# Attention output left transposed, its factors spread by loads through DRAM, dummy transposes ahead of the first layer norm, and a table of due times in the scheduler of an Infini-attention and GEGLU kernel

## The chip, the core and the metric

The kernel runs on one core of a Trainium2 chip. A core has five engines, each with its own queue of instructions executed in order: TensorE (PE in the profile, its weight loads PEld), VectorE (DVE), ScalarE (ACT), GpSimd (POOL) and SyncE (SP, which here only issues DMA). They synchronise by semaphores. PE writes to PSUM, which has eight banks of 128 partitions x 512 words of float32. The metric is the device time of one execution in microseconds; lower is better.

## The reference

One transformer layer over 2048 tokens of width 512: attention with 32 heads of 16 in four segments of 512 tokens with a memory that is carried from segment to segment, then a gated feed-forward of width 1376, each behind a layer norm and with a residual.

```python
for s in range(4):                     # segments
    logits = q_s @ k_s.T * 0.25 + mask # causal, per head
    a_dot = softmax(logits) @ v_s
    pq = phi(q_s)                      # phi(t) = t + 1 if t > 0 else exp(t)
    a_mem = (pq @ M) / (pq @ z + 1e-6)
    o_s = g * a_mem + (1 - g) * a_dot  # g = sigmoid(beta), one per head
    M += phi(k_s).T @ v_s;  z += phi(k_s).sum(0)
h = x + o @ wo
out = h + (gelu(ln(h) @ w_gate) * (ln(h) @ w_up)) @ w_down
```

## The kernel before, in words

The heads are worked on in four chunks of eight (`c`), the tokens in four segments (`s`). A pair is a unit `U`; there are 16, in the order of `UNITS`: all chunks of segments 0 and 1 first, then of 2 and 3. Each unit is worked on in two halves `Q` of four heads. What needs the float32 precision is split into two float32r parts, so a product is three matmuls (`SPLIT`).

The program is written as a list of operations, each with an engine, an estimated duration, a priority `prio` (a due time: the lowest goes first) and the tiles that it reads and writes. `Sched.run` goes through a modelled time, picks for each engine what is ready first, among those within a small window the one with the lowest `prio`, and so fixes the order of every engine's instructions; pools (`Pool_`) hand out tiles and PSUM banks in that order. The chip then executes these orders and waits on semaphores where the model was wrong. Before the change every `prio` is a formula in `U`, `Q` or `s`, such as `2 * U + (-2.08)`, and a DMA is modelled by a fixed delay (`lat`) behind its issue.

- `ln1(s)` loads four tiles of x (L517) and normalises them (`layer_norm`): for segments 0 and 1 on DVE (L450 to L471), for 2 and 3 with the sums on ACT (L436, L445). The result is transposed by PE (L497) and split by ACT and DVE (L506, L507) into `xt`.
- `qkv(U)` projects q and k (L536) and v (L565), copies q and k out of PSUM (L594, L596) and moves them by DMA into the layout of the score matmuls: `stq` (L609) and `stk` (L615). These buffers are first filled with zeros and ones by POOL and ACT (`c_fill` at L360, `c_stk` at L378 and L381). For segments 0 to 2 the keys' feature map goes, transposed (L632), into the memory product (L640), masked into `mb` (L643).
- `mem(U)`, for segments 1 to 3 (12 units): PE multiplies the memory with the queries (L664; tokens on partitions, 8 heads x 17 columns, the 17th being the denominator), DVE adds 1e-6, takes the reciprocal, multiplies by the gate and scales (L671 to L681) into `om`.
- `pass_a(Q)`: scores (L701) and their row maxima (DVE, L711), which go by DMA into a row of `stq` (L739). `pass_b(Q)`: transposed scores (L756) minus the maxima, exponentials on ACT (L760), causal masks on POOL (L764), and the product with v in four 32-column tiles of the array side by side (L785), which leaves in bank `pv` the result transposed: heads and their 16 values on partitions (the 17th row of each is the softmax sum), tokens on columns. ACT copies it out (`pvs`, L804), PE transposes it back in four transposes (L808), DVE takes the reciprocal of the sums, multiplies by 1 - g and scales (L820 to L824), POOL adds `om` (L829), and SP stores 128 KB to `o_dram`, token rows in runs of 256 bytes (L835).
- `wo_seg(s)` loads four tiles of `o_dram` and of x (L850, L851), transposes the first (L855), splits it (L506, L507), multiplies it with wo (L862), adds x on DVE (L866) and stores the residual (L868). Its operations' `prio` is `27.83 + 1.924 * s`, in the units of `U` and `Q`.
- The second layer norm and the feed-forward (L1031, L1092 on PE, weights prepared by ACT and POOL at L999 to L1008) fill the rest. From about 500 us on there is nothing else.

## Time and profile before

| | |
|---|---|
| Runs, us | 852.15, 851.84, 849.77; median 851.84 |
| Profiled execution, own time | 850.29 us |
| Its span (first to last instruction) | 848.2 us |
| Busy: PE, DVE, ACT, POOL | 825.0, 621.8, 511.7, 458.7 us |
| Share of 16 DMA engines, queue of SP | 34.8% |
| DMA moved | 82.9 MB, 64179 packets, 25056 of them under 512 bytes |

A row of the groups names the line, the engine, the operation, output and inputs, shapes, the number of instructions, then busy time and mean ns of one, then the idle time of the engine just before them and what ended it. A piece of the chain is start, length, and what it was. Matmuls overlap, so the mean of one is its latency and not the time that it adds. A float32 matmul stands as two records in the trace, a float32r one or a transpose as one.

### The profile page before, as it was taken

Reading aid. Unit: us, or ns where it says so; the run is one execution under the profiler, and the core shown is the slowest. Engines: PE = TensorE matmul, PEld = TensorE weight load, DVE = VectorE, ACT = ScalarE, POOL = GpSimd, SP = SyncE. Lnnn points to the kernel's source line nnn. Section 1 sums busy time; section 2 is a strip of 40 time slices with the busy share of each in tenths; the row PEclk is TensorE's granted clock in tenths of the full one; section 3 lists DMA queues with packets and bytes.
Section 4 is the critical chain, followed back from the end, with each engine's and each line's share of the span. In section 5 each row is a group of like instructions: output and inputs, shape, how many; then the busy total and the mean of one; then the engine's idle time right before and its main releaser. Section 6 shows DMA issues by size and latency. Waiting matters only on the chain.

```text
span 848.2 us, 15681 instructions
## 1 busy us (share of the span) xinstructions
PE 825.0 (97%) x4924; PEld 656.3 (77%) x4924; DVE 621.8 (73%) x1963; ACT 511.7 (60%) x966; POOL 458.7 (54%) x791
## 2 busy tenths in 40 slices
PE   4899999999999999999999999999999999999998
PEld 4787777877788777887777688788888877788886
DVE  7788877779867778868698675565666885756656
ACT  6767667578755666557445763774656764636441
POOL 6433534434335453445333673588878767779650
PEclk9999999999999999999999999999999999999999
DMA  7444432444344333243343464422212351122102
GB/s 248 120 119 96 96 74 69 108 103 96 85 121 122 89 85 97 48 121 90 107 122 122 126 230 143 122 72 63 63 51 62 119 158 38 50 63 62 51 1 100
DMA packets 64179, 82.90 MB, mean 98 GB/s; under 512 B 25056, under 2 KB 27040, under 8 KB 64096
## 3 DMA queue, kind: packets, MB, share of 16 engines
q1 hardware_dynamic: 64096, 81.91, 34.8%
q8 instruction: 39, 0.64, 0.3%
q14 instruction: 44, 0.36, 0.2%
HBM read 43.14 MB, written 12.58 MB: 66 GB/s over the span
## 4 chain that ended last, share of the span: by engine, by line
PE 92%; DVE 4%; ACT 2%; issue 1%; DMA 1%; SPq 0%; POOL 0%; ACTq 0%; DVEq 0%; POOLq 0%
PE bank L1031 24%; PE bank L1092 14%; PE bank L536 10%; PE bank L701 9%; PE bank L756 9%; PE bank L785 8%; PE bank L862 5%; PE bank L565 4%; PE bank L497 2%; PE bank L808 2%; PE bank L664 1%; PE bank L640 1%; PE bank L632 1%; PE bank L855 1%; ACT pt L760 1%
## 5 line engine op out<-in xcount | busy, mean ns | idle before, releaser
L711 DVE CUSTOM_DVE_ANT_0 junk<-bank,amask 128x256 f32<-128x256 f32 (+3 forms) x512 | 231.0, 486 | 54.1 <-PE bank L701 49.8
L764 POOL TENSOR_SCALAR_AFFINE_SELECT pt<-pt 128x128 f32<-128x128 f32 (+1 forms) x448 | 131.8, 314 | 202.5 <-ACT pt L760 192.1
L760 ACT ACTIVATE pt<-bank 128x512 f32<-128x512 f32 x320 | 177.8, 602 | 63.0 <-PE bank L756 50.4
L701 PE MATMUL bank<-stk,stq 128*128 128x512 f32 (+2 forms) x384 | 130.5, 386 | 0.9 <-DVE nm L711 0.5
L756 PE MATMUL bank<-stq,stk 128*128 128x384 f32 (+3 forms) x512 | 119.8, 325 | 1.3 <-ACT pt L760 0.8
L536 PE MATMUL bank<-xt,w 128*128 128x512 f32 x384 | 109.2, 397 | 0.0
L756 PEld LDWEIGHTS bank<-stq,stk 128*128 128x128 f32 x512 | 85.8, 189 | 15.4 <-ACT pt L760 6.2
L1097 DVE TENSOR_TENSOR pt<-pt,bank 128x512 f32<-128x512 f32 x96 | 64.9, 685 | 28.7 <-PE bank L1092 28.3
L701 PEld LDWEIGHTS bank<-stk,stq 128*128 128x128 f32 x384 | 66.8, 189 | 19.5 <-issue 9.3
L536 PEld LDWEIGHTS bank<-xt,w 128*128 128x128 f32 x384 | 70.0, 189 | 10.9
L785 PE MATMUL bank<-pt,vaug 128*32 128x512 f32 (+3 forms) x1024 | 76.0, 436 | 0.0
L785 PEld LDWEIGHTS bank<-pt,vaug 128*32 128x32 f32 x1024 | 28.4, 109 | 39.9 <-issue 31.8
L1001 POOL TENSOR_TENSOR w<-raw,w 128x512 fp32r<-128x512 f32 (+2 forms) x36 | 42.4, 1180 | 25.4 <-ACT w L999 24.1
L394 POOL TENSOR_TENSOR w<-raw,w 128x512 fp32r<-128x512 f32 (+1 forms) x26 | 34.1, 1312 | 40.6 <-ACT w L389 24.0
L1031 PE MATMUL bank<-xt,stk 128*128 128x512 f32 (+1 forms) x189 | 53.0, 394 | 0.3 <-ACT pq L1038 0.3
L565 PE MATMUL bank<-wv,xt 128*128 128x256 f32 x384 | 52.7, 284 | 0.0
L565 PEld LDWEIGHTS bank<-wv,xt 128*128 128x128 f32 x384 | 50.6, 190 | 1.1
L1031 PE MATMUL bank<-xt,w 128*128 128x512 f32 (+1 forms) x183 | 50.8, 391 | 0.0
L1001 POOL TENSOR_TENSOR stk<-raw,stk 128x512 fp32r<-128x512 f32 (+3 forms) x32 | 36.9, 1155 | 20.1 <-ACT stk L999 19.7
L804 ACT ACTIVATE pvs<-bank 128x512 f32<-128x512 f32 x32 | 19.2, 598 | 44.9 <-PE bank L785 44.9
L1031 PE MATMUL bank<-stk,w 128*128 128x512 f32 (+1 forms) x162 | 45.5, 392 | 0.0
L711 DVE DVE_READ_ACCUMULATOR2_ANT nm<- 128x1 f32 x512 | 42.2, 82 | 0.0
(271 smaller groups left out, 1731.3 us busy)
## 6 DMA issues: line engine op xcount, KB each, us to landing
stq<-hl SPq DMA_DIRECT2D x96, 128.0 KB
stk<-hl SPq DMA_DIRECT2D x192, 64.0 KB
row<-x SPq DMA_DIRECT2D x24, 256.0 KB
raw<-wg SPq DMA_DIRECT2D x20, 256.0 KB
raw<-wu SPq DMA_DIRECT2D x20, 256.0 KB
raw<-wd SPq DMA_DIRECT2D x20, 256.0 KB
o_dram<-o SPq DMA_DIRECT2D x32, 128.0 KB
row<-o_dram SPq DMA_DIRECT2D x16, 256.0 KB
```

What stands on the lines that cost most here:

```text
L536: nc.tensor.matmul(pm.t, w.t[:, wi, dc * P:(dc + 1) * P], XT[s][dc].t[:, xi, :], start=dc == 0 and n == 0, stop=dc == ND - 1 and n == 2)
L565: nc.tensor.matmul(pm.t[:, 256 * t:256 * t + 256], XT[s][dc].t[:, xi, t0:t0 + P], whl[wi].t[:, h, 256 * (dc % 2):256 * (dc % 2) + 256], st ...
L701: nc.tensor.matmul(sa.t[:, k * w:(k + n) * w].rearrange("x (n w) -> x n w", n=n), sq.t[:, p, i * P:(i + 1) * P], sk.t[:, p, a:a + n, 0:w], ...
L711: nc.vector.tensor_tensor_reduce(out=junk.t[:, :w], in0=sa.t[:, k * w:(k + 1) * w], in1=amask[:, D - w:], op0=OP.add, op1=OP.min, scale=-1 ...
L756: nc.tensor.matmul(sc.t[:, lo:lo + D - q0], sk.t[:, p, a, q0:q0 + P], sq.t[:, p, q0:D], start=True, stop=True)
L760: act(D, prio, lambda: nc.scalar.activation(e.t, sc.t, AF.Exp), [sc], [e])
L764: nc.gpsimd.affine_select(v, v, pattern=pat + [[1, P]], compare_op=OP.is_ge, fill=0.0, base=0, channel_multiplier=-1)
L785: nc.tensor.matmul(pv.t[32 * n:32 * n + 32, kb * P:D], va.t[:, kb, 17 * j:17 * j + 32], e.t[:, lo:lo + D - kb * P], start=kb == 0, stop=la ...
L1001: pool(0.14 + 2.13e-3 * (hi - lo), prio, lambda: nc.gpsimd.tensor_tensor(v.t[:, 1, :hi - lo], r.t[:, lo:hi], v.t[:, 0, :hi - lo].bitcast(F ...
L1031: nc.tensor.matmul(dst.t[:w], v.t[:, wi, c0 + j * w:c0 + (j + 1) * w], b[bk][j].t[:, xi, :], start=first and j == 0 and n == 0, stop=j == ...
L1092: nc.tensor.matmul(pm.t, HH[p, f, s][hi].t[:w, t * P:(t + 1) * P], v.t[:w, wi, :], start=f == fl[0] and n == 0, stop=f == fl[-1] and n == 2)
L1097: dve(D, prio, lambda a=a, pm=pm: nc.vector.tensor_tensor(a.t, a.t, pm.t, op=OP.add), [pm], [a])
```

## The change

**The result stays transposed.** ACT's copy of `pv` (`pvs`) is stored to DRAM for each half (L861). After the second half two loads bring back, for all eight heads, the 16 values of each on 128 partitions (`n`, 256 KB) and the sums in a small tile (`cd`) (L867). DVE takes the reciprocal of the sums and multiplies by 1 - g; SP stores them (L876) and a load with a stride of zero spreads each head's row over 16 partitions into `r` (`spread`, L736). POOL multiplies and, for segments 1 to 3, adds `om`; the tile is stored to `o_dram`, now transposed too (L883). `wo_seg` loads it as it is and splits it by ACT and POOL; there are no transposes left in either place. The rows of wo and beta are put in the matching order on the host.

**The memory read likewise.** One group of four 32-column matmuls gives the denominators (`den`, L713), DVE makes the factors (L718 to L720), they are stored and spread (L723, L736), one matmul of 512 columns gives the numerators with the tokens on columns (L729), which waits for the spread factors by the list of its inputs; DVE multiplies (L731). The mask of the memory product writes its columns in two pieces (`mask`).

**Dummy transposes.** 17 transposes of the fourth tile of x (L555) stand ahead of the first layer norm's on PE; nobody reads them. The fills of the third and fourth `stk` buffer wait for the second layer norm (`vcalm[1]`) instead of the first v projection.

**The scheduler.** The model of a transfer now lays transfers one behind another by size (`ring`) and holds SP when eight are outstanding. The pools change: `row` from 6 to 4 tiles, `o` and `cc` go, `n`, `r`, `cd`, `z` come. A table `DUE` holds 216 numbers, by unit, half or segment, that are added to the due times of q, k, v, the moves, the memory read, both passes, the accumulation, the output and the projection. So nearly every engine's order changes.

```diff
+DUE = {
+    "q": [0.25, 2.625, -4, 1, -1.25, 1.375, -0.625, -4, 0.25, -1.25, 2.125, 0.75, 0, 0.875, 0, 1.125],
...
+            if o.eng == "SP":
+                ring = max(ring, end) + o.lat
+                o.lat = ring + 1.5 - end
+                landed.append(ring + 1.5)
+                free["SP"] = max([end] + landed[-8:-7])
...
-        prio = 2 * UNIT[0, s] + (-4.21)
+        prio = 2 * UNIT[0, s] + (-4.21) + DUE["l"][s]
...
+        if s == 0:
+            wm = Val(PB)
+            pe(17 * 2 * TR, prio, lambda: [nc.tensor.transpose(
+                wm.t[:, (n % 4) * P:(n % 4 + 1) * P], rows[3].t[:, (n % 4) * P:(n % 4 + 1) * P],
+                ident) for n in range(17)], [rows[3], vident], [wm])
...
-        for n in range(2):
-            pm, cc = Val(PD), Val(PCC)
-            def f(n=n, pm=pm):
-                for t in range(2):
-                    nc.tensor.matmul(pm.t[:, 136 * t:136 * t + 136],
-                                     pq.t[:, (2 * n + t) * P:(2 * n + t + 1) * P], mb.t,
-                                     start=True, stop=True)
...
+        def den():
+            for t in range(4):
+                nc.tensor.matmul(pd.t[32 * t:32 * t + 32, 0:P], mb.t[:, P:160],
+                                 pq.t[:, t * P:(t + 1) * P], start=True, stop=True,
+                                 tile_position=(0, 32 * t), skip_group_check=True)
+        def inv():
+            nc.vector.tensor_scalar(pd.t[:, 0:P], pd.t[:, 0:P], 1e-6, None, op0=OP.add)
+            nc.vector.reciprocal(pd.t[:, 0:P], pd.t[:, 0:P])
+            nc.vector.tensor_scalar(z.t, pd.t[:, 0:P], gt[:, 1, c:c + 1], None, op0=OP.mult)
+        dma(prio, lambda: nc.sync.dma_start(
+            r_dram[U, 1].rearrange("j (t q) -> t j q", t=4), z.t[0:P:4]), [z], [vr], kb=16)
+        spread(prio, r, U, 1, vr)
+        pe(0.87, prio, lambda: nc.tensor.matmul(pm.t, mb.t[:, 0:P], pq.t, start=True, stop=True),
+           [pq, mb, r], [pm], acq=[om])
+        dve(D, prio, lambda: nc.vector.tensor_tensor(om.t, pm.t, r.t, op=OP.mult), [pm, r], [om])
+    def spread(prio, r, U, i, vr):
+        src = r_dram[U, i]
+        dma(prio, lambda: nc.sync.dma_start(r.t, bass.AP(
+            tensor=src.tensor, offset=src.offset, ap=[[0, 16], [D, 8], [1, D]])), [vr], [r], dur=0.67)
...
-        pe(4 * TR, prio, tr, [pvs, vident], [pn], acq=[cc, o])
+        dma(prio, lambda: nc.sync.dma_start(pv_dram[U, half], pvs.t), [pvs], [OUT[U]], chain=True)
+        if half == 0:
+            return
+        for first, ap, kb in ((16 * D, [32, 16], 24), (0, [D, 16], 256)):
+            dma(prio, lambda first=first, ap=ap: nc.sync.dma_start((cd if first else o).t, bass.AP(
+                tensor=src.tensor, offset=src.offset + first,
+                ap=[ap, [32 * D, 8], [1, ap[0]]])), [OUT[U]], [cd if first else o], kb=kb, dur=0.67)
+        def inv():
+            nc.vector.reciprocal(cd.t, cd.t)
+            nc.vector.tensor_scalar(cd.t, cd.t, gt[:, 0, c:c + 1], None, op0=OP.mult)
+        spread(prio, r, U, 0, vr)
+        pool(1.24, prio, lambda: nc.gpsimd.tensor_tensor(o.t, o.t, r.t, op=OP.mult), [r], [o])
+        if s:
+            pool(1.24, prio, lambda: nc.gpsimd.tensor_tensor(o.t, o.t, OM[U].t, op=OP.add),
+                 [OM[U]], [o])
...
-            pe(4 * TR, prio, tr, [ro, vident], [pt], acq=[ot])
-            split_psum(prio, pt, ot)
+            act(D, prio, lambda ro=ro, ot=ot: nc.scalar.activation(ot.t[:, 0], ro.t, AF.Copy), [ro],
+                [ot], src=0.092)
+            pool(1.23, prio, lambda ro=ro, ot=ot: nc.gpsimd.tensor_tensor(
+                ot.t[:, 1], ro.t, ot.t[:, 0].bitcast(F32), op=OP.subtract), [ro], [ot])
...
-            c_stk(2, [VA[0]])
-            c_stk(3, [VA[0]])
+            c_stk(2, [vcalm[1]])
+            c_stk(3, [vcalm[1]])
```

Three places show how the orders move. The first is ACT at the program's start, before: `xt` is what the first projection reads, `row_98` the first tile of x of segment 2, `stk_88` a buffer that is filled.

```order
L389 ACTIVATE w_82<-raw_105 128x512
L407 ACTIVATE wv_85<-raw_106 128x512
L378 ACTIVATE stk_88<-one 64x2x512
L506 ACTIVATE xt_73<-bank_65 128x512
L506 ACTIVATE xt_74<-bank_66 128x512
L506 ACTIVATE xt_75<-bank_67 128x512
L506 ACTIVATE xt_76<-bank_68 128x512
L378 ACTIVATE stk_88<-one 64x2x512
L436 ACTIVATE junk_118,bn_154<-row_98 128x512
```

And the same place of ACT now:

```order
L422 ACTIVATE w_82<-raw_103 128x512
L440 ACTIVATE wv_85<-raw_104 128x512
L469 ACTIVATE junk_116,bn_152<-row_98 128x512
L411 ACTIVATE stk_88<-one 64x2x512
L539 ACTIVATE xt_73<-bank_65 128x512
L539 ACTIVATE xt_74<-bank_66 128x512
L539 ACTIVATE xt_75<-bank_67 128x512
L539 ACTIVATE xt_76<-bank_68 128x512
L411 ACTIVATE stk_88<-one 64x2x512
```

The sum over `row_98` moved from behind the four copies to ahead of them, and with it ahead of a fill. The second place is POOL around the fills of the third and fourth `stk` (89 and 90), before:

```order
L369 MEMSET amask 128x512
L370 AFFINE_SELECT amask<-amask 128x128
L394 TENSOR_TENSOR w_83<-raw_105,w_83 128x512
L394 TENSOR_TENSOR w_84<-raw_106,w_84 128x512
L381 MEMSET stk_89 64x2x512 x2
L381 MEMSET stk_90 64x2x512 x2
L394 TENSOR_TENSOR w_81<-raw_104,w_81 128x512
```

And now, where `tick` is a one-column copy that waits for the normalised tile `pt_115`:

```order
L402 MEMSET amask 128x512
L403 AFFINE_SELECT amask<-amask 128x128
L427 TENSOR_TENSOR w_83<-raw_103,w_83 128x512
L427 TENSOR_TENSOR w_84<-raw_104,w_84 128x512
L562 COPY tick<-pt_115 128x1
L414 MEMSET stk_89 64x2x512 x2
L414 MEMSET stk_90 64x2x512 x2
```

The fills stand at the same place of POOL's queue, but behind an instruction that waits for the second normalisation. The third place is the memory read of the fourth unit (`mb_138` before, `mb_140` now) on PE, before:

```order
L756 MATMUL bank_70<-stq_94,stk_90 128x384
L756 MATMUL bank_70<-stq_94,stk_90 128x128
L701 MATMUL bank_69<-stk_88,stq_92 128x512
L701 MATMUL bank_68<-stk_88,stq_92 128x512
L664 MATMUL bank_67<-mb_138,pq_122 128x136 x2
L756 MATMUL bank_71<-stq_94,stk_90 128x384
L756 MATMUL bank_71<-stq_94,stk_90 128x128
```

Now on PE, from the denominators (L713) to the numerators (L729); what is left out between is the rest of the accumulation L838 and the scores of both passes:

```order
L576 MATMUL bank_65<-xt_75,w_81 128x512 x3
L713 MATMUL bank_66<-pq_120,mb_140 32x128 x4
L838 MATMUL bank_72<-pt_106,vaug_134 32x512
...
L809 MATMUL bank_70<-stq_94,stk_90 128x384
L809 MATMUL bank_70<-stq_94,stk_90 128x128
L729 MATMUL bank_66<-pq_120,mb_140 128x512
L809 MATMUL bank_71<-stq_94,stk_90 128x256 x2
```

And the transfers of that unit in SP's queue now:

```order
L663 DMA stq_93<-amask 4x4x256
L723 DMA r_dram<-z_129 4x8x128
L861 DMA pv_dram<-pvs_123 128x512
L736 DMA r_125<-r_dram 128x1x512
L883 DMA o_dram<-n_124 128x4x128
L652 DMA stq_94<-hl_95 32x2x512 x3
```

The matmuls of L664 needed only tiles that were on the chip; L729 needs `r_125`, whose load stands in SP's queue behind the store of `pvs_123`, the result of the accumulation L838 that PE does in between. In all PE has 2583 rows in its order for 2630, SP 502 for 378.

## The prediction

> **What bounds the kernel now.** I read the page first, then TensorE's waits, a table by stage, and the chain of waits piece by piece. The page gives the engines' busy time and the chain's shares:

> ```profile
> span 848.2 us, 15681 instructions
> PE 825.0 (97%) x4924; PEld 656.3 (77%) x4924; DVE 621.8 (73%) x1963; ACT 511.7 (60%) x966; POOL 458.7 (54%) x791
> PE 92%; DVE 4%; ACT 2%; issue 1%; DMA 1%; SPq 0%; POOL 0%; ACTq 0%; DVEq 0%; POOLq 0%
> ```

> TensorE (PE) is busy 97% of the span and 92% of the chain. The rest must be short. The stages (stretch, its length, PE's busy time, then the other engines, granted clock, DMA share, GB/s) and PE's longest waits say where it is:

> ```profile
> 0.00:10.70 10.70, 0.00 (x0) 0.01 (x1) 8.43 (x29) 6.22 (x7) 5.68 (x15) 1.00 0.81 280
> 10.70:14.70 4.00, 3.98 (x17) 3.24 (x17) 3.23 (x6) 1.68 (x3) 2.69 (x4) 1.00 1.00 366
> 50.00:475.00 425.00, 422.20 (x3046) 327.69 (x3044) 340.06 (x1446) 267.99 (x511) 178.10 (x493) 1.00 0.38 98
> 500.00:848.20 348.20, 343.59 (x1534) 279.67 (x1532) 224.02 (x371) 188.92 (x354) 235.23 (x225) 1.00 0.26 79
> PE bank L497 <- DVE pt L471: 12.4, 3, 10.7
> PE bank L808 <- DVE row L866: 2.1, 1, 2.1
> ```

> PE does nothing for 10.7 us while the first rows of x come in and are normalised, loses a little around 26 us and one wait of 2.1 us, and is otherwise fed. In the attention stretch (50 to 475) it is idle 2.8 of 425 us. So the time follows the PE work that is taken out, unless new waits arise. That is the frame of the sum.

> **The PE work that goes and comes.** Transposes and small matmuls as groups, and a piece of each from the chain (start, duration, what):

> ```profile
> L808 PE MATMUL bank<-ident,pvs 128*128 128x128 f32 x128 | 19.3, 273 | 2.1 <-DVE row L866 2.1
> L855 PE MATMUL bank<-ident,row 128*128 128x128 f32 x64 | 9.6, 272 | 0.0
> L664 PE MATMUL bank<-mb,pq 128*128 128x136 f32 x96 | 14.5, 280 | 0.0
> 100.07 2.29 PE bank L785 x32
> 103.38 0.44 PE bank L808 x4
> 397.90 0.44 PE bank L855 x4
> 398.34 0.47 PE bank L664 x4
> ```

> The groups' means (273 ns) are latencies of pipelined instructions, so I price by the chain's pieces, which lie end to end. Removed: 128 transposes of the attention result, 128/4 x 0.44 = 14.1 us; 64 transposes ahead of the output projection, 64/4 x 0.44 = 7.0; 96 records of the memory read, 96/4 x 0.47 = 11.3. Together 32.4 us.

> Added, for each of the 12 units that read memory: one matmul over 512 columns (L729) and a group of four 32-column matmuls over 128 (L713). The piece of L785 covers 512+384+256+128 = 1280 columns, four tiles beside each other, in 2.29 us, the piece of L664 2 x 136 columns in 0.47. The 512 columns are then 0.89 (by L664) to 0.92 (by L785); I take 0.90, 10.8 us in all. The 128 columns are 2.29/10 = 0.23, 2.7 us in all. The visits to the four-tile form stand apart in 34 places before and 39 after. The pair of matmuls behind a visit takes longer than twice a single one elsewhere:

> ```profile
> 102.36 0.55 PE bank L701 x2
> 104.74 0.23 PE bank L701
> ```

> 0.55 - 2 x 0.23 = 0.09 a visit, 5 x 0.1 = 0.5 us. Net: 32.4 - 10.8 - 2.7 - 0.5 = **18.4 us** less PE work. The 17 dummy transposes are no part of it: they need only the fourth row of x and lie in the first 10.7 us (cold, 17 x 0.27 = 4.6 us by the row of sixteen below). If that row came late they would delay the real transposes by at most that; between 6.7 us, when the fourth row is read, and 10.7 there are 4.0.

> The wait of 2.1 us at L808 is one of a transpose that asked for a bank while DVE had others in front. The transpose goes, and no matmul in its place needs that bank then: **-2.1**. What is late next there is the feed-forward's own work, which PE does without waits from 500 on.

> **The start.** Rows of the timeline, then two stretches:

> ```profile
> 6.55 3.29 SPq L517 DMA_DIRECT2D row<-x  x5
> 9.37 1.04 ACT L378 ACTIVATE stk<-one 64x1024 fp32r<-64x1024 f32 x1
> 10.03 1.92 DVE L471 TENSOR_SCALAR pt<-pt,mv,ln 128x512 f32<-128x512 f32 x4
> 10.72 4.31 PE L497 MATMUL bank<-ident,pt 128*128 128x128 f32 x16 [10.72 <-DVE pt L471]
> 12.51 0.60 ACT L506 ACTIVATE xt<-bank 128x512 fp32r<-128x512 f32 x1 [2.11 <-PE bank L497]
> 16.77 0.63 ACT L436 ACTIVATE junk<-row 128x512 f32<-128x512 f32 x1
> 24.44 4.45 POOL L381 MEMSET stk<- 64x1024 f32 x4
> 24.88 4.29 DVE L471 TENSOR_SCALAR pt<-pt,mv,ln 128x512 f32<-128x512 f32 x4
> 43.70 3.73 SPq L615 DMA_DIRECT2D stk<-hl  x6
> 26.50:29.00 2.50, 0.99 (x3) 0.42 (x3) 2.50 (x3) 1.59 (x3) 2.29 (x3) 0.99 0.59 134
> 29.00:32.40 3.40, 3.05 (x11) 2.51 (x12) 2.40 (x8) 1.76 (x3) 0.00 (x0) 0.50 0.49 118
> 15.30:20.50 5.20, 5.20 (x24) 4.30 (x23) 4.47 (x11) 4.41 (x8) 5.06 (x13) 1.00 0.39 108
> ```

> Three things change. First, the transposes: sixteen take 4.31 us here and would take 4 x 0.44 = 1.8 on a warm array. The first four are paced by the normalisation (ends at 11.95), so a warm array saves about 1.3 us.

> Second, ScalarE (ACT). The sum of the ninth tile's row, row_98 (before it ran at 16.77), now stands ahead of a fill of stk and of the copy that PE's first projection waits for. That row is the twelfth load of 256 KB: 3.15 MB, of which 280 GB/s x 10.7 us = 3.0 MB are in at 10.7 us and the rest by 11.1, to which some completion time comes; I take 12.0. The sum (0.63 and about 0.2 to read it out) and the fill (1.04, which before ran at 9.37 in ACT's spare time) then end at 13.9 to 14.0, so the copy moves from 12.51 to about 14.0. The four copies no longer wait for cold transposes, but the projection starts some 0.7 us later (-0.4 to 1.5). The warm transposes' gain is inside this figure: the ACT order eats it.

> Third, GpSimd's (POOL) four fills of stk run at 24.44 beside DVE's second normalisation, which takes 4.29 us where the same four instructions took 1.92 before: 2.4 us, and PE waits there. In the stretch of 3.4 us behind that gap the granted clock is 0.50, up to 1.7 us more. The new order puts these fills behind the normalisation, so they end near 32; the transfers into these buffers, which need them, were issued at 43.7 before (the SP row), so the fills stay hidden. I credit 3.0 of 2.4 + 1.7 = 4.1, since PE arrives later by the 0.7. Start in sum: **-2.3** (bounds -4.5 to +1.5).

> [...]

> **The way through DRAM.** The factors that were applied in the transposed layout now go by DMA: two stores of the result, two gathers, a store of the reciprocals, a load that spreads them over 16 partitions, for memory units a second such pair. SyncE (SP) issues 502 rows in the place of 378. One hop alone, and SP's load:

> ```profile
> 446.59 3.32 DMA row<-o_dram
> stq<-hl SPq DMA_DIRECT2D x96, 128.0 KB
> stk<-hl SPq DMA_DIRECT2D x192, 64.0 KB
> o_dram<-o SPq DMA_DIRECT2D x32, 128.0 KB
> 102.26 4.73 SPq L615 DMA_DIRECT2D stk<-hl  x6
> SPq L835 <- POOL pt L764: 43.7, 13, 6.0
> ```

> A load took 3.32 us from issue to use. The result's path is six hops, 20 us, and some 4 us of ACT, DVE and POOL; the order leaves 24 us of PE work (added up at the prices of this part) between the last accumulation of the 15th unit and the projection of its segment, and 38 at the 16th: just covered the first time.

> The memory path is two hops and three DVE instructions, 6.6 + 1.5 (an estimate: two of 0.3 and a reciprocal between) = 8 us. The new matmul L729 waits for it in PE's queue, with all PE work behind it. Between the two PE steps of the fourth unit stand an accumulation (2.29), sixteen 512-column matmuls (0.23 each) and smaller ones, 7.5 us; at the sixth unit 10, at the ten others 15 to 40. So there are three tight places, of 0 to 3.3 us each (one slipped hop): I take **+2**, bounds 0 and 10.

> The DMA engines are no bound: 4.2 MB of stores go and about 24 MB come, so about 20 MB more in 425 us, 47 GB/s on the 98 of the attention row, whose share of 0.38 rises to 0.56 at most. POOL gets 28 multiplications and additions and 16 subtractions of 512 columns for the 24 additions of 256:

> ```profile
> L829 POOL TENSOR_TENSOR o<-o,om 128x256 f32<-128x256 f32 x24 | 17.8, 741 | 23.9 <-DVE o L824 22.4 <-DVE mm L727 0.7 <-DVE ln L466 0.6
> ```

> At twice 0.74 at most that is 44 x 1.48 - 17.8 = 47 us on 459, of a span of 848: no bound either. DVE loses the three operations behind each group of transposes and gets fewer.

> **The due times.** They reorder everything between 31 and 500 us. PE's hidden loss there can be seen in like pieces of unlike length:

> ```profile
> 98.03 0.53 PE bank L756 x4
> 109.94 0.47 PE bank L756 x4
> ```

> 512 matmuls of L756 are 128 such pieces; if half lose 0.06 that is 4 us, L701 about as much, idle 2.8 on top: some 10 us in all that a better order could give back, and a worse one could double. In the new order the uses of ACT's and DVE's pairs of banks stand a little further apart: added up at the prices above, what they fall short of 1.5 us of PE work is 17 us in all against 20. I take **-3** (-10 to +10).

> **The sum.** 848.2 - 18.4 - 2.1 - 2.3 + 2 - 3 = 824.4 us of span. The profiled run's own time is 850.29, 2.1 above its span: 826.5. It lies 1.55 below the median of the runs (851.84), so the forecast is **828** us.

> **The rivals.**

> *The order gives more back:* if the 10 us of hidden and open loss in attention go and no transfer is late, 828 - 7 - 2 = 819. For it: many due times are free now. Against it: such pieces are paced by ACT's 0.60 us for each bank (as in L506's row), which stays.

> *Transposes do not warm the array:* then the first projection's matmuls run at half pace until a stretch of 3.4 us (the one seen at clock 0.50) is over, +1.7: 829.7. This is the case in which the change does not do what it says. The rows of 10.7 to 20.5 us speak against it. [...]

> *Late factors at the short gaps:* if the three tight places wait a whole hop each, 828 - 2 + 3 x 3.3 = 836. SP's rows for it: a store of the result, which waits for the accumulation and ACT's copy, stands between the store of the factors and the load that spreads them.

> *Slower:* the same wait at all 12 memory units. L729 stands in PE's queue in order, so each wait stops PE; at 3.3 us each it is 40 us, 828 + 38 = 866. It decides from (851.84 - 826)/12 = 2.2 us a unit (826 is the forecast without the 2). SP's L835 row shows that it already stands 43.7 us behind stores. Against it: at ten of the twelve the gap is nearly twice the 8 us or more.

> **Chances.** Forecast 0.60, more given back 0.15, no warming 0.07, short gaps 0.11, slower 0.07. Range 817 to 841: from the better order to the short gaps with the start's worst bound on top; it leaves out the slower case and little of the others. A measurement of this kernel can tell about 0.3%, 2.6 us: faster 0.91, same 0.02, slower 0.07.

> **What would show it.** PE's busy time should fall to about 805 to 811 (825 - 18.4, plus up to 4.6 for the dummies); the rows of L808 and L855 are gone. L504's four instructions near 25 us should take about 2 us, no stretch at clock 0.50 behind them. The first copy of xt (L539) should start near 14 and the first projection near 15.4. PE's waits should name L729 behind a DMA r<-r_dram, in total under 5 us. I am wrong if the attention stretch shows PE idle for over 10 us, or if the projection's L910 waits for row<-o_dram.

## The result, and the profile after

The changed kernel takes **845.72 us** (median of 4 runs, 844.19 to 845.77), the kernel before 851.38 (4 runs, 849.77 to 852.15): ratio 0.9923, 95% interval 0.9908 to 0.9939 (the two medians alone give 0.9934, inside it). It is faster by 0.7 to 0.8%, as the direction of the forecast had it, but 828 us was forecast, with a range of 817 to 841: of the 24 us that were to be gained, 6 came. The profiled execution's span is 842.5 us, 18.1 over the 824.4 of the sum.

First the page of the changed kernel, the three rows that answer to those of before.

```profile
span 842.5 us, 15436 instructions
PE 815.5 (97%) x4773; PEld 636.7 (76%) x4773; DVE 614.6 (73%) x1847; ACT 511.3 (61%) x966; POOL 493.9 (59%) x813
PE 84%; DVE 6%; POOL 3%; DMA 2%; issue 2%; ACT 2%; SPq 0%; POOLq 0%; DVEq 0%; ACTq 0%
```

PE still is the bound, but its share of the chain fell from 92 to 84%: the chain now runs through other engines for 16% of the span. The stages say where. The stretches of the changed kernel, then two of before that the prediction does not show (columns: stretch, length, busy time of PE, PEld, DVE, ACT, POOL, granted clock, DMA share, GB/s):

```profile
50.00:475.00 425.00, 417.35 (x2964) 312.95 (x2967) 334.57 (x1313) 280.57 (x537) 212.50 (x521) 0.99 0.53 147
...
400.00:500.00 100.00, 95.17 (x575) 68.19 (x568) 82.32 (x262) 66.17 (x123) 70.89 (x126) 0.97 0.54 167
500.00:830.00 330.00, 325.45 (x1431) 263.80 (x1430) 211.28 (x344) 182.17 (x339) 234.62 (x225) 0.99 0.25 77
```

```profile
400.00:500.00 100.00, 96.68 (x625) 72.25 (x626) 80.74 (x272) 57.46 (x107) 49.81 (x107) 1.00 0.45 137
500.00:830.00 330.00, 329.19 (x1472) 268.07 (x1471) 213.05 (x354) 186.53 (x350) 235.23 (x225) 1.00 0.26 77
```

PE is idle 7.65 us of the attention stretch (2.8 before) and 4.6 us of 500 to 830, where it had been idle 0.8 before. What it waited for, by releaser (total, times, longest):

```profile
PE bank L576 <- DVE xt L540: 2.0, 1, 2.0
PE bank L530 <- DVE mx L790: 1.9, 1, 1.9
PE bank L530 <- DVE pq L939: 1.7, 1, 1.7
PE bank L809 <- DMA stq<-mx: 1.5, 2, 1.1
PE bank L1082 <- POOL xt L950: 1.5, 1, 1.5
PE bank L787 <- DVE mm L783: 1.5, 3, 0.6
PE bank L809 <- ACT pt L813: 1.4, 4, 0.6
```

Neither L729 behind the factors nor L910 behind row<-o_dram is among them: the way through DRAM is hidden (L910's one listed wait, 0.8 us at 499.7, is for POOL's split of a row, L905). The two longest waits outside the start stand at transposes (L530), at 412.9 and at 670.7. Both are followed by a stretch of 3.41 us at half clock, at 416.97 and at 676.4 (a third, at 468.2, follows three waits of 0.8, 0.4 and 0.4 us); the first, with the stretch ahead of it:

```profile
413.50:416.95 3.45, 1.47 (x7) 0.90 (x7) 3.45 (x13) 0.60 (x1) 2.71 (x4) 1.00 0.36 112
416.97:420.38 3.41, 3.28 (x10) 2.70 (x11) 3.41 (x18) 1.40 (x3) 1.67 (x3) 0.50 0.59 171
```

Around 412.9 the timeline shows DVE and POOL side by side (start, duration, engine, line):

```profile
405.29 1.28 POOL L1052 TENSOR_TENSOR w<-raw,w 128x512 fp32r<-128x512 f32 x1 [1.14 <-ACT w L1050]
...
405.31 1.28 DVE L496 TENSOR_TENSOR ln<-ln,ln 128x4 f32<-128x4 f32 x1
...
410.88 0.67 DVE L783 TENSOR_TENSOR mm<-nm,mm 128x16 fp32r<-128x16 f32 x1
...
412.14 2.86 DVE L522 TENSOR_SCALAR row<-row,mv,ln 128x512 f32<-128x512 f32 x4
...
412.28 1.53 POOL L1052 TENSOR_TENSOR w<-raw,w 128x512 fp32r<-128x512 f32 x1
...
414.92 0.27 DVE L790 COPY mx<-bank 32x128 f32<-32x128 f32 x1
...
415.25 0.66 PE L530 MATMUL bank<-ident,row 128*128 128x128 f32 x4 [1.93 <-DVE mx L790]
```

An instruction of DVE on four elements a partition takes 1.28 us, exactly as long as POOL's subtraction that began 0.02 us ahead of it; the median of the twelve of its kind is 0.16. The normalisation L522 takes 2.86 for four tiles: one by one in the trace 0.53, 1.50, 0.54 and 0.54, the second beside POOL's subtraction at 412.28. L790, for which PE waits, stands behind them. In kernels whose order is the same up to here, PE's wait at this place is 1.9 us (here, e6 and e10) to 3.4 (e5), so single profiles scatter by more than 1 us.

The second place, in the feed-forward's second half:

```profile
641.41 1.75 SPq L1189 DMA_DIRECT2D row<-h_dram  x4
...
668.08 1.31 POOL L427 TENSOR_TENSOR w<-raw,w 128x512 fp32r<-128x512 f32 x1 [5.44 <-ACT w L422]
...
672.74 0.66 PE L530 MATMUL bank<-ident,row 128*128 128x128 f32 x4 [1.74 <-DVE pq L939]
...
675.43 0.74 PE L1082 MATMUL bank<-xt,stk 128*128 128x512 f32 x2 [1.53 <-POOL xt L950]
```

The second four rows of h are loaded at 641.4 only, when the first four's transposes have given their buffers back: the change cut the row pool from six to four. Before, only two of them were loaded so late:

```profile
652.46 0.80 SPq L1138 DMA_DIRECT2D row<-h_dram  x2
```

Now the layer norm of all four runs late, in ACT's and DVE's queues between the feed-forward's own work, POOL stands idle 5.44 us behind ACT, and its subtraction L950 comes late for PE.

The start went as forecast:

```profile
6.62 3.86 PE L555 MATMUL bank<-ident,pt 128*128 128x128 f32 x17 [6.62 <-DMA pt<-x]
10.48 3.00 PE L530 MATMUL bank<-ident,pt 128*128 128x128 f32 x16
12.56 0.63 ACT L469 ACTIVATE junk<-row 128x512 f32<-128x512 f32 x1 [2.83 <-DMA row<-x]
...
13.19 1.04 ACT L411 ACTIVATE stk<-one 64x1024 fp32r<-64x1024 f32 x1
...
14.14 2.02 ACT L539 ACTIVATE xt<-bank 128x512 fp32r<-128x512 f32 x4
...
15.49 2.79 PE L576 MATMUL bank<-xt,w 128*128 128x512 f32 x11 [2.01 <-DVE xt L540]
```

The copy starts at 14.14 (forecast 14.0), the projection at 15.49 (15.4), for the reason given: the sum L469 and the fill L411 stand ahead of the copy. The second normalisation (L504, at 26.12) takes 1.91 us for its four tiles where it took 4.29, and no stretch at half clock follows it (the clock's records show full clock from 10.79 to 416.97), as forecast too.

**One measure for all runs.** To compare orders that differ everywhere, I count what PE loses: for each pair of its instructions that follow each other, the time from start to start less the first one's undisturbed pace (0.228 us for 512 columns, 0.175, 0.119 and 0.060 for 384, 256 and 128, 0.109 for a transpose, 0.110 for 512 columns of the four-tile form, 0.430 for L729), added up by stage. Priced so, PE's work is 792.8 us before and 775.6 after, 1.85 of it dummies: 19.0 less (18.4 forecast). The last column counts how far DVE's instructions lie over the lower quartile of their line and shape (where over 0.06 us).

| | PE loses, 0-50 | 50-400 | 400-500 | 500 to end | sum | span | DVE lengthened |
|---|---|---|---|---|---|---|---|
| before | 8.2 | 21.2 | 9.9 | 1.3 | 40.7 | 848.2 | 13.9 |
| after | 8.6 | 23.5 | 16.2 | 7.8 | 55.9 | 842.5 | 19.9 |
| e1 four rows, table zero | 8.2 | 27.7 | 22.1 | 8.5 | 66.4 | 852.7 | 13.0 |
| e5 after, rows apart | 8.3 | 25.7 | 16.3 | 1.8 | 52.1 | 838.7 | 20.1 |
| e11 six rows, table zero | 8.3 | 27.5 | 19.2 | 3.0 | 58.0 | 845.0 | 17.7 |
| e14 six rows, table | 8.3 | 29.5 | 14.3 | 2.3 | 54.4 | 840.8 | 25.0 |
| e16 six rows, table | 8.8 | 27.2 | 16.0 | 1.3 | 53.3 | 839.8 | 26.9 |
| e18 planner knows POOL, zero | 7.9 | 29.3 | 13.4 | 1.3 | 52.1 | 838.9 | 13.9 |
| e15 planner knows POOL, table | 10.1 | 26.0 | 7.8 | 2.1 | 46.1 | 832.5 | 14.8 |
| e17 planner knows POOL, table | 8.2 | 26.9 | 9.6 | 1.6 | 46.3 | 832.8 | 15.7 |

So the gain was made and given back: 19.0 us of PE work and 1.85 at the start went, and 2.3 (50-400), 6.3 (400-500) and 6.5 (from 500 on) came. Kernels with the same order up to 400 (e5, e6, e9 and others) lose between 23.3 and 25.9 there, so a difference of 1 or 2 us in one profile says nothing. Nor does the last column alone tell the loss: e1 has the least lengthening and the largest sum.

### The profile page after: what moved, and what is told of

The parts are those of the page before. It is cut to its first block, busy times and chain, and to the rows that moved or that the text cites. A ratio compares the mean times of both kernels' runs of the same rounds, so it can differ in the third digit from the quotient of the medians.

```text
span 842.5 us, 15436 instructions
## 1 busy us (share of the span) xinstructions
PE 815.5 (97%) x4773; PEld 636.7 (76%) x4773; DVE 614.6 (73%) x1847; ACT 511.3 (61%) x966; POOL 493.9 (59%) x813
## 4 chain that ended last, share of the span: by engine, by line
PE 84%; DVE 6%; POOL 3%; DMA 2%; issue 2%; ACT 2%; SPq 0%; POOLq 0%; DVEq 0%; ACTq 0%
PE bank L1082 22%; PE bank L1143 13%; PE bank L576 9%; PE bank L754 9%; PE bank L809 9%; PE bank L838 8%; PE bank L605 5%; PE bank L910 5%; DVE junk L764 2%; PE bank L683 1%; PE bank L729 1%; PE bank L530 1%; POOL raw L1059 1%; DMA row<-x 1%; DMA stq<-mx 1%
## 5 line engine op out<-in xcount | busy, mean ns | idle before, releaser
L764 DVE CUSTOM_DVE_ANT_0 junk<-bank,amask 128x384 f32<-128x384 f32 (+3 forms) x512 | 227.7, 486 | 46.2 <-PE bank L754 44.0
L813 ACT ACTIVATE pt<-bank 128x512 f32<-128x512 f32 x320 | 177.7, 599 | 58.8 <-PE bank L809 49.5
L754 PE MATMUL bank<-stk,stq 128*128 128x512 f32 (+2 forms) x384 | 128.8, 387 | 1.1 <-DVE nm L764 0.7
L809 PE MATMUL bank<-stq,stk 128*128 128x384 f32 (+3 forms) x512 | 118.9, 324 | 3.1 <-DMA stq<-mx 1.5
L809 PEld LDWEIGHTS bank<-stq,stk 128*128 128x128 f32 x512 | 86.3, 190 | 20.1 <-ACT pt L813 7.2
L576 PEld LDWEIGHTS bank<-xt,w 128*128 128x128 f32 x384 | 68.1, 188 | 13.0 <-DVE xt L540 2.2
L838 PE MATMUL bank<-pt,vaug 128*32 128x512 f32 (+3 forms) x1024 | 76.7, 436 | 0.0
L838 PEld LDWEIGHTS bank<-pt,vaug 128*32 128x32 f32 x1024 | 28.4, 109 | 36.5 <-issue 30.6
L605 PE MATMUL bank<-wv,xt 128*128 128x256 f32 x384 | 54.9, 283 | 0.0
L605 PEld LDWEIGHTS bank<-wv,xt 128*128 128x128 f32 x384 | 52.5, 189 | 2.4 <-DVE xt L540 0.2
L1082 PE MATMUL bank<-xt,w 128*128 128x512 f32 (+1 forms) x180 | 51.7, 402 | 0.0
L1082 PE MATMUL bank<-xt,stk 128*128 128x512 f32 (+1 forms) x156 | 44.5, 398 | 2.1 <-POOL xt L950 1.5
L879 POOL TENSOR_TENSOR n<-n,r 128x512 f32<-128x512 f32 x16 | 21.0, 1311 | 40.3 <-DMA r<-r_dram 32.6
L764 DVE DVE_READ_ACCUMULATOR2_ANT nm<- 128x1 f32 x512 | 42.2, 82 | 0.0
L1052 POOL TENSOR_TENSOR w<-raw,w 128x512 fp32r<-128x512 f32 (+2 forms) x33 | 38.0, 1154 | 4.9 <-ACT w L1050 4.8
L1052 POOL TENSOR_TENSOR stk<-raw,stk 128x512 fp32r<-128x512 f32 (+3 forms) x30 | 35.0, 1170 | 9.8 <-ACT stk L1050 9.2
## 6 DMA issues: line engine op xcount, KB each, us to landing
stq<-hl SPq DMA_DIRECT2D x96, 128.0 KB
```

The costliest lines, as they stand in the source:

```text
L576: nc.tensor.matmul(pm.t, w.t[:, wi, dc * P:(dc + 1) * P], XT[s][dc].t[:, xi, :], start=dc == 0 and n == 0, stop=dc == ND - 1 and n == 2)
L605: nc.tensor.matmul(pm.t[:, 256 * t:256 * t + 256], XT[s][dc].t[:, xi, t0:t0 + P], whl[wi].t[:, h, 256 * (dc % 2):256 * (dc % 2) + 256], st ...
L754: nc.tensor.matmul(sa.t[:, k * w:(k + n) * w].rearrange("x (n w) -> x n w", n=n), sq.t[:, p, i * P:(i + 1) * P], sk.t[:, p, a:a + n, 0:w], ...
L764: nc.vector.tensor_tensor_reduce(out=junk.t[:, :w], in0=sa.t[:, k * w:(k + 1) * w], in1=amask[:, D - w:], op0=OP.add, op1=OP.min, scale=-1 ...
L809: nc.tensor.matmul(sc.t[:, lo:lo + D - q0], sk.t[:, p, a, q0:q0 + P], sq.t[:, p, q0:D], start=True, stop=True)
L813: act(D, prio, lambda: nc.scalar.activation(e.t, sc.t, AF.Exp), [sc], [e])
```

## The experiments

My theory after the result: the PE work fell as forecast and came back at two places, the joint of attention and feed-forward (400 to 500) and the second half's layer norm. Rivals: the searched due times lose it in attention; the added transfers delay the small ones; a lucky or unlucky order. All ratios are to runs of the kernel before on the same chip; the changed kernel's is 0.9923.

**The table set to zero (e1).**

```diff
+DUE = {k: [0] * len(v) for k, v in DUE.items()}
```

> The changed kernel with every entry of the DUE table set to zero: the transposed path, the dummy transposes and the planner's transfer model stay, only the order is another. PE's work is the same as after the change (its nominal sum 775.6 us). Theory A (the table is worth something, and the return path through DRAM would cost more without it): PE idle in 50 to 475 over the 7.65 us of the changed kernel, above 15 us, with waits of L729 behind its DMA; time 852 to 862 us. Theory B (the table itself brought the loss; my forecast credited it with 3 us and the trace shows 2.3 lost before 400 us and 8 between 400 and 500): idle under 7 us there, time 836 to 843 us.

Measured: 853.89 us, ratio 1.0036 (1.0021 to 1.0051). Theory B falls: the table gains 8.2 us over none (9.6 by the ratios), and without the table the change is slower than the kernel before. PE's idle time at the joint is twice that of the changed kernel (stretch as above):

```profile
400.00:500.00 100.00, 90.30 (x537) 62.81 (x530) 73.35 (x235) 55.34 (x102) 60.01 (x106) 0.97 0.54 160
```

Theory A's time is met, its mechanism is not: PE idles 12.4 us in 50 to 475, not over 15, and L729 is not in PE's list; the longest waits there are for DVE (L765, 4.8 us in all) and ACT (L814, 3.9).

**Without the dummies (e2).**

```diff
-                ident) for n in range(17)], [rows[3], vident], [wm])
+                ident) for n in range(0)], [rows[3], vident], [wm])
```

> The changed kernel in its own order, but without the 17 dummy transposes (left out: they compute nothing that is used). If transposes count for the clock: the clock becomes full some 3.9 us of transposes later, the sixteen transposes of L530 take 4.3 us instead of 3.0 and the first projection starts at 15.5 to 16.5; time 846.5 to 848.5 us. [...]

Measured: 847.84 us, ratio 0.9961 (0.9948 to 0.9975). The weight loads of its transposes and of its first projection:

```profile
11.88 2.55 PEld L530 LDWEIGHTS bank<-ident,pt 128*128 128x128 f32 x13 [0.28 <-DVE pt L504]
15.27 3.31 PEld L576 LDWEIGHTS bank<-xt,w 128*128 128x128 f32 x15 [0.85 <-DVE xt L540]
```

and the same thirteen with the dummies ahead of them (the changed kernel):

```profile
11.84 1.40 PEld L530 LDWEIGHTS bank<-ident,pt 128*128 128x128 f32 x13 [0.32 <-DVE pt L504]
```

Thirteen transposes take 1.40 us with the dummies ahead of them and 2.55 without, 0.108 and 0.196 each; the records of the clock begin with full clock at 10.79 with the dummies and at 14.27 without, each time after some 4 us of nothing but transposes. In the kernel before, too, PE did nothing but transposes from 10.7 to 14.7, and in 15.3 to 20.5 its 24 matmuls took 5.2 us, 0.217 each. So in each of these profiles the faster pace came behind some 4 us of transposes. But the projection starts no sooner with them (15.49 against 15.27), since ACT's copy paces it in both (it starts at 14.14 and at 13.92). The 2 us by which this kernel is slower do not lie in the start; its profile shows 2.4 more lost in 50-400 (inside the scatter of equal orders named above) and 1.0 more behind 500, in the same order. What the dummies have to do with that is open.

**POOL short at the joint (e3), DVE short (e9), ACT in DVE's place (e4), ACT short (e10).** In e3 POOL's work on the first two tiles' weights runs over 8 columns, in e9 DVE's L522, in e10 the last exponentials run over 256; in e4 the sums and the normalisation go to ACT.

```diff
+        def cut(k):
+            return 8 if (p, f) in todo[:2] else k
...
-                v.t[:, 1, :hi - lo], r.t[:, lo:hi], v.t[:, 0, :hi - lo].bitcast(F32), op=OP.subtract),
+                v.t[:, 1, :cut(hi - lo)], r.t[:, lo:lo + cut(hi - lo)],
...
+                k = 8 if dst[0] else D
...
-                    rows[t].t, rows[t].t, mv.t[:, t, 0:1], y.t[:, t:t + 1], op0=OP.subtract,
+                    rows[t].t[:, :k], rows[t].t[:, :k], mv.t[:, t, 0:1], y.t[:, t:t + 1], op0=OP.subtract,
...
-    OFF = (False, False)
+    OFF = (True, False)
...
+            k = 256 if Q == 31 else D
+            act(D, prio, lambda: nc.scalar.activation(e.t[:, :k], sc.t[:, :k], AF.Exp), [sc], [e])
```

> The changed kernel in its own order, but GpSimd's subtractions and sums for the first two feed-forward tiles' weights touch 8 columns in the place of 64 to 512 (left out: the rest of these low parts and combinations). Theory P (GpSimd's tensor_tensor lengthens DVE's instructions that read SBUF, by some 3 us in 400 to 425, and that makes PE wait 2.09 us at 412.9 with a half-clock window of 3.4 us behind it): the wait falls under 0.5 us, the window is gone, time 841.5 to 843.5 us (-2 to -4). Rival (DVE is full there by its own work, 24.5 of 25 us): the wait stays over 1.5 us and the time within 1 us of 845.7.

> The changed kernel in its own order, but DVE's four normalisations of the feed-forward's first rows (L522) touch 8 columns in the place of 512 (left out: the rest of these rows' normalisation). Theory: DVE's own 2.86 us there stand ahead of L790 and make PE wait 1.9 us at 412.9, with the half-clock window behind it: the wait falls under 0.3 us, no window of 3.4 us near 417, time 842 to 843 us. Rival (what e3 showed with the wait halved: the next link, the store of mx and L809 behind it, takes its place): PE waits over 1 us for L809 behind the store at 414 to 418, the window stays, time 844.5 to 846 us.

> The changed kernel with the sums and the normalisation of the first layer norm of the feed-forward (first 512 rows) on ScalarE instead of DVE (OFF = (True, False)); nothing moves before about 400 us. If DVE's fullness in 400 to 425 causes the 2.09 us wait and the half-clock window: both go, time 841 to 844 us. Rival (ScalarE, which paces the banks of pass b at 0.6 us each, takes the place of DVE): PE waits for ScalarE by L809 and L530, time 846 to 851 us.

> The changed kernel in its own order, but ScalarE's ten exponentials of the last pass b (L813) touch 256 columns in the place of 512 (left out: the other half of these exponentials). Theory: ScalarE's 0.54 us for each of the dense banks of the last pass make PE wait 0.8, 0.4 and 0.4 us at 464 to 468, with the half-clock window at 468.2 behind them: the waits fall under 0.2 us each, the window goes, time 842.5 to 844 us. Rival (the window follows from something else than these waits, or the wait moves to DVE): time within 1 us of 845.7.

Measured: e3 843.86 us, 0.9917 (0.99 to 0.9934); e9 844.23, 0.9926 (0.9908 to 0.9943); e4 851.09, 1.0004 (0.9991 to 1.0016); e10 845.63, 0.9939 (0.9918 to 0.9959). By the ratios none gains clear of the intervals. In e3 the wait for L790 is 0.7 us in the place of 1.9, and the next link (L809 behind the store of mx) takes as much, as these rows of the waits between 411 and 418 show:

```profile
PE bank L809 <- DMA stq<-mx: 0.7, 1, 0.7
PE bank L530 <- DVE mx L790: 0.7, 1, 0.7
```

In e9 DVE's four normalisations on 8 columns still took (timeline)

```profile
412.92 1.83 DVE L523 TENSOR_SCALAR row<-row,mv,ln 128x8 f32<-128x8 f32 x4
```

and PE still waited 0.9 us for L790. One by one the four took 0.28, 1.25, 0.28 and 0.28 us: the second met a subtraction of POOL of 1.27. In e3, with POOL short, the four took 1.90 on all 512 columns. So of the 2.86 us about 1 is the columns' own work and about 1 is POOL beside one of the four. The same shows in the changed kernel at L496, whose two inputs are both in SBUF: 1.28 us for four elements beside a POOL subtraction of 1.28, 0.16 without one. In e10 the half-clock stretch at 468.2 is gone, but 0.66, 0.41 and 0.41 us are still lost there and the time isn't less. In e4 PE idles 7.5 us in 400 to 500 (4.8 after the change); its longest waits there are for ACT (L813, 1.5 us in all, 1.2 after the change) for DVE (L764 1.5, L588 1.2) and for POOL (L905 1.2), so it is not ACT alone that takes DVE's place.

**The second group's rows in buffers of their own (e5).** Nothing moves before about 560 us.

```diff
-                    rows = [Val(PROW) for _ in range(4)]
+                    rows = [Val((PROW, PC)[s]) for _ in range(4)]
```

> The changed kernel, but the second group of rows of the feed-forward's second half takes four free buffers of another pool (PC) in the place of the row pool that the change cut to four; nothing moves before about 560 us. Theory R (the cut pool makes the second group load only after the first group's transposes, at 641, so that its layer norm, its transposes and POOL's part of xt stand late together): the waits of 1.9 us at 670.7 (L530 behind DVE) and 1.8 at 673.4 (L1082 behind POOL) go, and the half-clock window of 3.4 us behind them; time 839.5 to 842 us (-4 to -6). Rival (the second half's layer norm is late because of ACT's and DVE's queues whatever the buffers): the two waits stay over 1 us each and the time is within 1 us of 845.7.

Measured: **840.11 us**, ratio 0.9875 (0.9854 to 0.9895). Theory R holds: both waits and the half-clock stretch behind them are gone, and the stretch from 500 on is as full as before the change:

```profile
500.00:830.00 330.00, 329.13 (x1458) 267.36 (x1457) 212.26 (x352) 182.13 (x342) 237.70 (x227) 1.00 0.27 79
```

By the ratios the cut of the pool costs 0.48%, 4.1 us, at this place; by the medians it is 5.6 us, by the losses behind 500 6.0.

**Less POOL work in attention (e6), shorter transfers (e7).**

```diff
-        pool(1.24, prio, lambda: nc.gpsimd.tensor_tensor(o.t, o.t, r.t, op=OP.mult), [r], [o])
+        pool(1.24, prio, lambda: nc.gpsimd.tensor_tensor(
+            o.t[:, :8], o.t[:, :8], r.t[:, :8], op=OP.mult), [r], [o])
...
-        src = r_dram[U, i]
+        src, w = r_dram[U, i], D if U < 4 else 16
```

> The changed kernel in its own order, but GpSimd's 28 multiplications and additions of the attention result (L879, L881) touch 8 columns in the place of 512 (left out: the rest of the result). Theory P (GpSimd beside DVE is what costs in attention: DVE's instructions are 6 us longer in sum than before the change): PE's loss in 50 to 400 falls from 23.5 to the 21.2 of before or less, time 842 to 844 us. Rival (what is lost there is the order and the transfers): within 1 us of 845.7.

> The changed kernel in its own order, but from the fifth unit on the loads that spread the factors and gather the result bring 16 columns in the place of 512 (34 loads of 256 KB, 8.7 of the 20.6 MB that the change added; left out: the rest of these factors and results). Theory D (the added transfers delay the small ones that PE waits for: L809 behind the store stq<-mx, 1.28 us at 205 and 0.6 at 104): those waits fall under 0.3 us, PE's loss in 50 to 400 falls by 1.5 to 3 us, time 842 to 844. Rival (the small store's own latency sets these waits): within 1 us of 845.7, the wait at 205 over 1 us.

Measured: e6 844.27 us, 0.9921 (0.9903 to 0.994); e7 846.44, 0.9947 (0.9929 to 0.9966). Both rivals hold by the time (e6 by its ratio; its median lies between the two ranges): PE loses 24.0 and 23.3 us in 50-400, as without the edits. Neither the multiplications nor the bytes of the new transfers cost anything in attention that shows beside the scatter of 23.3 to 25.9. In e7 PE's waits behind stq<-mx did fall, from 1.5 to 0.4 us, as theory D had it, but this did not come back as time.

**A row of the table moved by 0.03 (e8).**

```diff
+DUE["p"] = [a + (0.03, -0.03)[i % 2] for i, a in enumerate(DUE["p"])]
```

> The changed kernel with the 32 entries of one row of the table (p, the accumulations) moved by 0.03 up and down in turn, less than a quarter of the table's own step of 0.125; the order is the same to about 200 us and another behind that. If the time hangs on the order in detail (the table's order is one good draw): the attention and the joint to the feed-forward lose 2 to 6 us more, time 848 to 852 us. If due times matter only in the large: within 1 us of 845.7.

Measured: 853.77 us, ratio 1.0024 (1.001 to 1.0038): 8 us for nothing but another order, all that the table gains over zero. The expectation was 848 to 852; the loss is larger still, 27.1 in 50-400 and 22.6 in 400-500. Against these two other orders (e1, e8) the table is one good draw.

**Six rows, table zero (e11).**

```diff
-    PROW = Pool_(many("row", 4, [P, D]), fifo=True)
+    PROW = Pool_(many("row", 6, [P, D]), fifo=True)
```

> The kernel of e1 (table zero) with the row pool at six buffers as before the change. If the cut of the row pool is what makes the path without the table slower than before (e1: 853.9): PE's loss in 400 to 500 falls from 22.1 us to 10 to 16, the second half's layer norm loses under 3 us, time 843 to 848 us. Rival (the order of the new path with untuned due times, not the buffers): time 850 to 854 us.

Measured: 846.66 us, ratio 0.9951 (0.9934 to 0.9969): 7.2 us better than with four rows (e1); by the losses 5.5 less behind 500, as expected, and 2.9 less in 400-500, where 19.2 are left and 10 to 16 were expected. Without any table six rows do nearly what four rows and the table do. Six rows with the change's own table were not run.

**All three places at once (e12), DVE and POOL short (e13).** Edits as above.

> The changed kernel with three edits together: the second group's rows in buffers of their own (e5), the four normalisations at 8 columns (e9), the last pass's exponentials at 256 columns (e10). If the three places are what separates the forecast from the result and they add up: 840.1 (e5) less 2 to 3.5 at 412.9 and less 1.5 to 3 at 464, that is 833.5 to 836.5 us. If a wait taken away at one place comes back at the next: 839 to 841 us.

> The kernel of e5 (second group's rows apart) with the edits of e3 and e9 together: POOL's work on the first two feed-forward tiles' weights and DVE's four normalisations of the first rows touch 8 columns (left out: the rest of both). Theory (DVE's instructions stand while POOL's tensor_tensor runs, whatever their own size: four of 8 columns took 1.83 us in e9): with both short the wait for L790 at 412.9 falls under 0.4 us and no window at clock 0.50 follows near 417; time 836 to 838 us (840.1 less 2 to 4). Rival (the chain of small steps from L764 to the store of mx sets it): a wait of over 0.8 us stays at 412 to 418, time 839 to 841 us.

Measured: e12 837.9 us, 0.985 (0.9828 to 0.9872); e13 837.17, 0.9842 (0.9825 to 0.986). e12 lies between its two expectations: of the 3.5 to 6.5 us hoped for at the joint some 2 came. In e13 the four short normalisations take 0.90 us instead of 1.83, and PE's transposes (L531 there) start without a wait; the next link is late again:

```profile
411.13 0.90 DVE L523 TENSOR_SCALAR row<-row,mv,ln 128x8 f32<-128x8 f32 x4
...
412.53 0.66 PE L531 MATMUL bank<-ident,row 128*128 128x128 f32 x4
...
416.50 1.22 PE L810 MATMUL bank<-stq,stk 128*128 128x512 f32 x2 [1.61 <-DMA stq<-mx]
```

The time is inside the theory's range (836 to 838), but the signs are the rival's: the stretch at half clock stays (at 416.3), and PE waits 1.61 us for the store of mx, the end of a chain of small steps (L764, L783, L790) that follows close behind. PE loses 6.4 us in 400 to 430, against 7.6 to 8.9 in six profiles without an edit there (the changed kernel, e2, e5, e6, e7, e10). So POOL and DVE's own columns hold the start of these transposes at 412.9, but taking both away gives back only some 1 to 2.5 us of this place.

**Six rows and tables searched for them (e14, e16), and a planner that knows POOL (e15, e17, e18).** The search moves entries of the table and keeps what shortens the plan; e14 to e18 also have the edit of e5, and four entries more for the layer norms' and two for the first weights' due times. The planner of e15, e17 and e18 has these lines more (psum marks the pools of PSUM banks; busy is POOL's last long instruction). They put in what was measured beside POOL's tensor_tensor: 1.28 us for 0.16 at L496, 1.25 for 0.28 in e9, and 0.67 to 0.69 as ever at L1108 with an operand in PSUM:

```diff
+            if o.eng == "DVE" and at < busy[1] and not any(v.pool and v.pool.psum for v in o.vals):
+                end = busy[1] + o.dur
+            if o.eng == "POOL" and o.dur > 0.9:
+                busy = (at, end)
```

> Six row buffers, the second group's rows apart as in e5, and another table of due times, searched for six rows. If cut and table add (the table gains over zero what it gained at four rows, 853.9 - 845.7 = 8.2): 846.7 - 8.2 = 838.5, some 836 to 841 us. If the table only made good what the cut of the row pool cost: 845 to 848 us.

> As e14, but the planner that orders the instructions lets a DVE instruction without a PSUM operand begin behind POOL's running tensor_tensor, and its table was searched with this. If DVE standing behind POOL is a good part of what is lost at the joint: PE's loss in 400 to 500 falls under 8 us (16.2 after the change), time 1 to 4 us under e14. If it is not: within 1 us of e14.

> As e14 (the planner doesn't know that DVE stands behind POOL), with a table searched as long as that of e15. If the knowledge counts: 838 to 845 us, and DVE's instructions are lengthened beside POOL by 20 us or more in sum, as in e14 (25.0 by the same count; 14.8 in e15). If the longer search made e15's gain: 831 to 836 us.

> As e15, with another table (204 of its 234 entries differ). If e15's gain comes from the planner's knowledge: 830 to 836 us. If it was a lucky order: 837 to 845 us, about as far from e15 as e8 was from the changed kernel.

> As e11 (six rows, table zero) with the second group's rows apart (e5) and the planner of e15, no table. e11 lost 2.3 us in the feed-forward, of which the rows apart may give 1. If the knowledge counts without a search too: 838 to 843 us. If it only helps a search: 844 to 848 us.

| | planner blind | planner knows POOL |
|---|---|---|
| table zero | e11 846.66, 0.9951 (0.9934 to 0.9969) | e18 840.61, 0.9883 (0.9867 to 0.99) |
| searched | e14 843.21, 0.9918 (0.9892 to 0.9944) | **e15 832.8, 0.9788 (0.9765 to 0.9812)** |
| searched again | e16 841.55, 0.9891 (0.9876 to 0.9906) | e17 835.09, 0.9816 (0.9801 to 0.9831) |

The stretch of 400 to 500 in e16, e15 and e18:

```profile
400.00:500.00 100.00, 93.44 (x561) 67.38 (x561) 81.15 (x231) 58.79 (x108) 63.77 (x115) 0.97 0.56 173
```

```profile
400.00:500.00 100.00, 97.64 (x599) 72.19 (x599) 82.33 (x244) 65.73 (x125) 73.48 (x130) 1.00 0.57 177
```

```profile
400.00:500.00 100.00, 94.19 (x572) 67.81 (x565) 78.41 (x237) 58.03 (x108) 65.49 (x111) 1.00 0.58 177
```

With the same buffers and a table the knowledge gives 6.5 to 10.4 us (e16 to e17, e14 to e15); without a table 6.1, of which e5's edit, which e11 has not, is 1.7 by the losses behind 500. (For e15 only 1 to 4 us had been expected; e17's table has 222 entries, not the 234 of its expectation, and 204 of them differ from e15's.) PE's loss at the joint falls to 7.8 and 9.6 us, DVE is lengthened by 14 to 16 us in the place of 25 to 27. A longer search alone (e14 to e16) gives 1.7 us, inside the intervals. e14 falls between its two expectations: cut and table don't simply add. That the new lines give better orders is shown with two tables and with none; that they do so by POOL's hold on DVE, and not by a slower DVE in the model as such, is argued from the lengthening and not tested. e15 is the best version: 2.1% under the kernel before and, by the ratios, 1.4% under the changed one.

## Why the direction was right and the size wrong

Point by point, against the prediction's terms (span):

- **PE work, -18.4: right.** 19.0 less by PE's own pace. The rows of L808 and L855 are gone. PE's busy time fell only to 815.5 and not to 805-811, since it counts an instruction's whole time, at half clock or held up by its inputs too (so I read it; the pace is the better count).
- **Start, -2.3: right.** -1.85: the first PE instruction starts 4.1 us sooner, 1.85 are dummies, 0.4 more is lost. That ACT's order eats the warm transposes' gain was right to 0.14 us. The rival of no warming fell (e2: 0.108 us for a transpose behind the dummies, 0.196 without them), but for the same reason it would have cost nothing at the projection.
- **Factors through DRAM, +2: too much.** L729 is not among PE's listed waits, and PE loses at most 0.09 us ahead of any of the twelve; the rivals of late factors and of waits at all 12 units fell. Shorter transfers gain nothing that shows (e7).
- **Wait of 2.1 us at L808, -2.1: the step failed.** The wait itself went with its transposes. But I wrote that what is late next there is the feed-forward's own work, which PE does without waits. It is the layer norm in front of it and the last pass of attention: PE waits at 412.9 behind DVE's normalisation, one of whose four tiles takes 1.50 us beside POOL and the others 0.53 to 0.54, then (e3, e13) for the store of mx, and at 464 to 468 for ACT's exponentials. 400-500 loses 6.3 us more instead of 2.1 less. How the 6.3 divide is open: the short instructions of e13 and e10 take away some 1 to 2.5 and 1.7 us of loss.
- **Row pool, not priced: the step that was missing.** The cut from six to four stood in the diff, and I put it at nothing without a reason. It costs 4.1 to 6.0 us in the second half (e5) and 7.2 us in all where no table works around it (e1, e11).
- **Due times, -3: failed.** I judged the order by how far the uses of ACT's and DVE's banks stand apart. The table does gain, 8.2 us over none; but set against the old order, attention lost 2.3 us more and the joint 6.3. The planner whose order the table steers doesn't have POOL's hold on DVE (1.28 us for 0.16 at L496); with it, six rows and other tables the same path takes 832.8 to 835.1 us (e15, e17).

The direction was in part luck: with the table at zero (e1) or moved by 0.03 (e8) the same change, with its four rows, is slower than the kernel before, and the forecast had priced neither the row pool nor new waits at the joint.

By the losses: 3.3 us of the 18.1 that are missing lie in 50-400 (2.3 found, -1 forecast), 8.4 in 400-500 (6.3 and -2.1), 6.5 behind 500, 0.5 in the start, 0.3 at the end, less 0.7 of PE work. The sign I had named for being wrong, PE idle over 10 us in attention, was not reached (7.65); a bound for 400 to 500 and one for the feed-forward were missing.

Open: why every order of the new path loses 23 to 29 us in 50-400 where the old one lost 21.2. Neither POOL's multiplications (e6) nor the bytes of the transfers (e7) do it as far as the scatter lets one see. What the dummies gain outside the start is open too.

## What to carry to other kernels

A change that takes work from the engine at its limit is worth that work only if every buffer that it shrinks is followed to its last user: here two row buffers cost 4 to 7 of 19 us, most of it in a stage that the change doesn't touch otherwise. A searched order can be a draw that fits one graph and one model (here 0.03 on some entries cost 8 us): before searching longer, look in the trace for what the model does not know, here DVE standing behind POOL (1.28 us for 0.16 at L496), and put that in.

## What the runs showed of the hardware

- DVE's instruction on 128x4 elements in SBUF (L496 of the changed kernel, twelve cases) took 1.28 us beside POOL's tensor_tensor of 1.28, and 0.16 to 0.23 in the eleven others; of e9's four on 128x8 the one that met a POOL tensor_tensor of 1.27 took 1.25 and the others 0.28 each; in e13, where POOL's work was short, all four took 0.28 to 0.33.
- The same multiplication on DVE (L1108 of the changed kernel, 512 columns) took 0.67 to 0.69 us in all its 22 cases with the second operand in a PSUM bank, with POOL beside it or not. With both operands in SBUF it took 0.69 in the four cases without POOL beside it and 0.69 to 3.16 in the eighteen with POOL. Two of its groups in the changed kernel (the mean of the first holds one case without POOL):

```profile
L1108 DVE SCALAR_TENSOR_TENSOR ge<-ge,vaug 128x512 f32<-128x512 f32 x5 | 6.9, 1378 | 0.1
...
L1108 DVE SCALAR_TENSOR_TENSOR ge<-ge,bank 128x512 f32<-128x512 f32 x2 | 1.4, 681 | 0.0
```
